# A fused linear-attention and multiplicative-FFN kernel: Strassen block products, an earlier weight product, and a list-scheduled order

## The chip, the cores and the metric

The kernel runs on one core of one Trainium2 chip. The metric is the device time of one execution in microseconds (us). Every median below is over the executions of that kernel in one comparison (three to eight). Executions come in a fast and a slow state; for one core an execution counts as slow when it is over 1.5% above the fastest of its kernel.

Engines: PE is TensorE (matmuls and transposes), ACT is ScalarE, DVE is VectorE, POOL is GpSimd, SP is SyncE, whose queue issues the DMAs. PEld is PE's weight load.

## The reference

Eight batches of 576 tokens, 8 heads of 64 features: q, k, v are (8, 8, 576, 64) in float32. The attention is a linear one, and its result feeds a multiplicative FFN.

```python
q_s = exp(q - max(q, -1)); q_s /= sum(q_s, -1)          # softmax over the features of a token
k_s = exp(k - max(k, 2));  k_s /= sum(k_s, 2)           # softmax over the tokens
kv  = einsum('bhsd,bhse->bhde', k_s, v)                 # 64x64 per head
x   = einsum('bhsd,bhde->bhse', q_s, kv)                # -> 4608 tokens x 512 features
a, b = x @ w1, x @ w2                                   # 4608 x 1024 each
out  = ((a * b) @ w3) @ w_out                           # 4608 x 512
```

## The kernel before

It computes in float16 with float32 accumulation, and multiplies w3 @ w_out once into `W3O`, so that the last two products become one. Tokens go through in nine chunks of 512. For each chunk, `s1` makes a block of 128 of the 1024 features with eight matmuls of 512 columns, ACT copies the first product out of PSUM, DVE multiplies it into the second; `s2` makes the output. The pieces of later batches' attention are woven by hand between the feature blocks.

```python
def load_qkv(b, which, hf):                     # half of the heads of q, k or v of a batch
    t = slot([SP, 4, R * D])                    # 96 partitions, 4 runs of 1536 B in each
    nc.sync.dma_start(out=t, in_=src[b, 4*hf:4*hf+4].rearrange("h (p r) d -> p h (r d)", r=R))

def piece_t(b, p):                              # transpose the normalised q on PE, DVE copies it out
    pt = pAtt([P, R, SP], F16)
    for r in range(R):
        nc.tensor.transpose(pt[:, r, :], eqn[:, r]..., ident[:SP, :SP])
    nc.vector.tensor_copy(out=qsT, in_=pt...)

def s1(j, fb):
    pa = pAB()
    for ct in range(4):
        nc.tensor.matmul(pa, lhsT=w1sb[qt][:, ct, fo:fo + P], rhs=xT[ct][:, t0:t0 + 512], ...)
    nc.scalar.copy(out=a16, in_=pa)
    pb = pAB()
    for ct in range(4):
        nc.tensor.matmul(pb, lhsT=w2sb[qt][:, ct, fo:fo + P], rhs=xT[ct][:, t0:t0 + 512], ...)
    nc.vector.tensor_tensor(out=ab, in0=pb, in1=a16, op=ALU.mult)

# order: q, k, v of batch 0; w1, w2; chunk 0; then w3 @ w_out; then chunks 1 to 8, in each of them
# the attention of batch j+1, the exponentials of batch j+2 and the loads of batch j+3
```

The softmax here doesn't subtract the row's maximum and nothing guards it: scores larger than these inputs give would overflow.

## Time and profile before

Median 292.8 us (291.25 to 293.15). In a window table a row is a stretch of time, and after it the busy time of each engine with its number of instructions, the granted PE clock, the busy share of the 16 DMA engines and what they moved in GB/s.

The first lines are from the page of the profile: PE's busy time, then the span in 40 slices of 7.26 us (a digit is the busy tenths of a slice) for PE, its granted clock and DMA, and the chain of work that ended last, by engine.

```profile
...
PE 245.5 (85%) x1440; PEld 125.1 (43%) x1440; DVE 140.0 (48%) x268; ACT 124.3 (43%) x217; POOL 79.2 (27%) x64
...
PE   0218997739693399999999999999999999999993
...
PEclk9999999998888579999999999999999999999999
DMA  7999999990139999949946965971121112121124
...
PE 79%; DMA 8%; ACT 5%; DVE 3%; issue 1%; SPq 1%; DVEq 0%; ACTq 0%
...
```

Counting the slices from 0, PE starts late, has holes in slices 6 to 13, and is full from slice 14 on. DMA is busy early and has room later. The next view is a table of stretches of the same execution.

```profile
...
core 0: us, PE busy (x) PEld busy (x) DVE busy (x) ACT busy (x) POOL busy (x), PEclk, DMA share, GB/s
40.00:60.00 20.00, 16.37 (x116) 8.67 (x115) 6.22 (x10) 6.93 (x10) 4.54 (x4) 1.00 1.07 296
80.00:100.00 20.00, 10.00 (x48) 4.27 (x47) 6.52 (x12) 9.08 (x16) 4.87 (x4) 0.76 0.78 191
120.00:140.00 20.00, 20.00 (x130) 10.57 (x129) 13.48 (x27) 11.52 (x22) 8.70 (x6) 1.00 0.75 181
160.00:180.00 20.00, 20.00 (x129) 10.50 (x128) 12.03 (x26) 10.33 (x19) 7.28 (x5) 1.00 0.72 179
...
```

From 110 us on PE is busy all the time at full clock. The waits of PE (line, what it waited for, total us, times, longest) show what the early holes are:

```profile
...
PE att L152 <- POOL v_0_75 L127: 10.0, 1, 10.0
PE att L180 <- DVE qsT L172: 7.8, 2, 5.4
PE att L169 <- POOL eqn L138: 7.7, 3, 3.9
PE pab L204 <- ACT a_880 L201: 5.9, 1, 5.9
PE att L235 <- ACT w_611 L232: 4.5, 1, 4.5
...
```

These are single long waits for the first batches and for w3. The first line is the time before PE's first matmul. A useful account of PE can be made from the starts of its matmuls. Take the time from one matmul's start to the next: up to the full-rate duration it is *work*; what the granted clock explains beyond that is *cold*; the rest is *waits*. For the full-rate duration the Trainium skill, "TensorE: Matmul & The Clock Gate", Part 1, gives columns / 2.4 + 2.5 ns; the spacing of 0.216 us at 512 columns in this trace agrees, and so does its half clock after idle stretches (the granted clock is 0.50 from 92 to 96 us, 0.76 on average from 80 to 100 us). About 5 us of tail and the time before the first matmul come on top. For this kernel: 231.1 us work, 6.6 cold, 38.4 waits, first matmul at 10.0 us.

### The profile page before, as it was taken

To read this page: it belongs to the slowest core of one execution; us is meant where nothing else is said; L and a number is where in the kernel's file an instruction comes from. 1 tells how busy PE (TensorE), PEld (TensorE's weight loads), DVE (VectorE), ACT (ScalarE), POOL (GpSimd) and SP (SyncE) were. 2 spreads that over 40 slices of the span, in tenths; PEclk is the share of its full clock that TensorE was granted. 3 is DMA by queue.
4 is the path that set the end of the run, shared out by engine and by line. 5 is a ranking of instruction groups with operands and counts; after the bars stand their busy time and mean duration, and the time that the engine had idled before them with its cause. 6 is when DMAs were issued, how large, how long until landed. Compare 5 with 4: busy or idle time off the path is not lost.

```text
span 290.4 us, 3985 instructions
## 1 busy us (share of the span) xinstructions
PE 245.5 (85%) x1440; PEld 125.1 (43%) x1440; DVE 140.0 (48%) x268; ACT 124.3 (43%) x217; POOL 79.2 (27%) x64
## 2 busy tenths in 40 slices
PE   0218997739693399999999999999999999999993
PEld 0115444415441155555555455455555544444441
DVE  0344453231733468476476476657745434333441
ACT  3426542263344558556464456445622332121200
POOL 1461702305503456354125405505400000000000
PEclk9999999998888579999999999999999999999999
DMA  7999999990139999949946965971121112121124
GB/s 182 254 326 391 357 351 282 261 250 15 41 97 236 256 256 256 228 118 220 280 129 156 257 149 128 261 208 38 48 62 38 36 47 64 36 73 38 55 76 121
DMA packets 31443, 48.49 MB, mean 167 GB/s; under 512 B 2240, under 2 KB 24768, under 8 KB 31424
## 3 DMA queue, kind: packets, MB, share of 16 engines
q1 hardware_dynamic: 31424, 48.24, 62.3%
q8 instruction: 11, 0.18, 0.3%
q14 instruction: 8, 0.07, 0.1%
HBM read 38.80 MB, written 9.44 MB: 166 GB/s over the span
## 4 chain that ended last, share of the span: by engine, by line
PE 79%; DMA 8%; ACT 5%; DVE 3%; issue 1%; SPq 1%; DVEq 0%; ACTq 0%
PE pab L204 22%; PE pab L198 21%; PE po L215 21%; DMA st<-in_q_dram 8%; PE po L243 5%; PE att L152 4%; PE att L180 3%; PE att L169 2%; ACT eq L120 2%; ACT ek L111 1%; PE att L235 1%; DVE ds L134 1%; SPq L78 1%; DVE osb L218 0%; ACT w_542 L232 0%
## 5 line engine op out<-in xcount | busy, mean ns | idle before, releaser
L138 POOL TENSOR_TENSOR eqn<-eq,dr 96x768 f16<-96x768 f16 x32 | 46.8, 1470 | 98.9 <-DVE dr L136 57.5
L134 DVE TENSOR_REDUCE ds<-eq 96x12 f32<-96x768 f16 x32 | 30.0, 936 | 44.2 <-ACT eq L120 44.1
L215 PEld LDWEIGHTS <-abT 128*128 128x128 f16 x288 | 27.6, 99 | 30.5 <-issue 1.1
L218 DVE TENSOR_SCALAR osb<-po 128x512 f32<-128x512 f32 x36 | 24.8, 688 | 27.2 <-PE po L215 26.2
L120 ACT ACTIVATE eq<-st 96x768 f16<-96x768 f32 x32 | 26.4, 843 | 11.8 <-DMA st<-in_q_dram 11.8
L111 ACT ACTIVATE ek<-st 96x768 f16<-96x768 f32 x32 | 25.8, 843 | 8.5 <-DMA st<-in_k_dram 8.5
L169 PE MATMUL att<-ident,eqn 96*128 96x96 f16 x192 | 14.8, 219 | 7.7 <-POOL eqn L138 7.7
L152 PEld LDWEIGHTS <-ek 96*128 96x128 f16 x192 | 14.5, 108 | 13.9 <-ACT ek L111 7.0
L169 PEld LDWEIGHTS <-eqn 96*128 96x128 f16 x192 | 12.4, 105 | 13.9 <-POOL eqn L138 8.7
L152 PE MATMUL att<-v_0_75,ek 96*128 96x130 f16 x96 | 8.8, 254 | 10.0 <-POOL v_0_75 L127 10.0
L172 DVE COPY qsT<-att 128x576 f16<-128x576 f16 x32 | 14.2, 450 | 0.7 <-PE att L169 0.6
L204 PEld LDWEIGHTS <-w_0_85 128*128 128x128 f16 x72 | 7.4, 103 | 16.0 <-issue 8.6
L127 POOL CAST v_0_75<-st 96x1536 f16<-96x1536 f32 x8 | 11.7, 1461 | 9.2 <-DMA st<-in_v_dram 8.8
L215 PE MATMUL po<-W3O_93,abT 128*128 128x512 f16 x36 | 13.9, 386 | 0.0
L215 PE MATMUL po<-W3O_96,abT 128*128 128x512 f16 x36 | 13.9, 386 | 0.0
L215 PE MATMUL po<-W3O_95,abT 128*128 128x512 f16 x36 | 13.9, 385 | 0.0
L215 PE MATMUL po<-W3O_94,abT 128*128 128x512 f16 x36 | 13.9, 385 | 0.0
L215 PE MATMUL po<-W3O_97,abT 128*128 128x512 f16 x36 | 13.7, 381 | 0.0
L215 PE MATMUL po<-W3O_98,abT 128*128 128x512 f16 x36 | 13.6, 379 | 0.0
L215 PE MATMUL po<-W3O_99,abT 128*128 128x512 f16 x36 | 13.6, 379 | 0.0
L215 PE MATMUL po<-W3O_100,abT 128*128 128x512 f16 x36 | 13.6, 379 | 0.0
L204 PE MATMUL pab<-xT_71,w_0_85 128*128 128x512 f16 x18 | 7.3, 404 | 5.9 <-ACT a_880 L201 5.9
(265 smaller groups left out, 507.3 us busy)
## 6 DMA issues: line engine op xcount, KB each, us to landing
st<-in_k_dram SPq DMA_DIRECT2D x16, 576.0 KB, 9.7
st<-in_v_dram SPq DMA_DIRECT2D x16, 576.0 KB, 8.5
st<-in_q_dram SPq DMA_DIRECT2D x16, 576.0 KB, 10.0
st<-in_moe_w_dram SPq DMA_DIRECT2D x16, 512.0 KB, 7.7
out_dram<-osb SPq DMA_DIRECT2D x24, 192.0 KB, 2.3
out_dram<-osb SPq DMA_DIRECT2D x24, 128.0 KB, 2.3
st<-in_moe_w_out_dram SPq DMA_DIRECT2D x4, 512.0 KB, 5.5
out_dram<-osb SPq DMA_DIRECT2D x24, 64.0 KB, 2.0
```

What stands on the lines that cost most here:

```text
L111: nc.scalar.activation(out=ek.rearrange("p r h d -> p h r d"), in_=t[:, o:o + 2].rearrange("p h (r d) -> p h r d", r=R), func=AF.Exp)
L120: nc.scalar.activation(out=eq.rearrange("p r h d -> p h r d"), in_=t[:, o:o + 2].rearrange("p h (r d) -> p h r d", r=R), func=AF.Exp)
L134: nc.vector.tensor_reduce(out=ds, in_=eq, axis=AX.X, op=ALU.add)
L138: nc.gpsimd.tensor_tensor(out=eqn.rearrange("p r h d -> p (r h) d"), in0=eq, in1=dr[:, :, None].broadcast_to([SP, 2 * R, D]), op=ALU.mult)
L152: nc.tensor.matmul(kvp[:, pp, :].rearrange("p (h e) -> p h e", h=2), lhsT=ek[:, r].rearrange("p h d -> p (h d)"), rhs=v16buf[b % 2][:, 2 * ...
L169: nc.tensor.transpose(pt[:, r, :], eqn[:, r].rearrange("p h d -> p (h d)"), ident[:SP, :SP])
L172: nc.vector.tensor_copy(out=qsT, in_=pt.rearrange("p r s -> p (r s)"))
L198: nc.tensor.matmul(pa, lhsT=w1sb[qt][:, ct, fo:fo + P], rhs=xT[ct][:, t0:t0 + CH], start=(ct == 0), stop=(ct == N_CT - 1))
L204: nc.tensor.matmul(pb, lhsT=w2sb[qt][:, ct, fo:fo + P], rhs=xT[ct][:, t0:t0 + CH], start=(ct == 0), stop=(ct == N_CT - 1))
L215: nc.tensor.matmul(po, lhsT=abT[(j, ft)][:, tb * P:(tb + 1) * P], rhs=W3O[ft], start=(ft == 0), stop=(ft == N_FT - 1))
L218: nc.vector.tensor_scalar(out=osb, in0=po, scalar1=ISC, scalar2=None, op0=ALU.mult)
L243: nc.tensor.matmul(wps, lhsT=w3Ts[ft][:, gt, :], rhs=wosb[gt // 2][:, gt % 2, :], start=(gt == 0), stop=(gt == N_FT - 1))
```

## The change

Its intent: (1) multiply x with w1 and w2 with seven block products instead of eight for all tokens but the first 512, (2) do w3 @ w_out first, while the attention's inputs load, (3) transpose q of batches 2 to 7 by DMA instead of by PE, (4) let a list scheduler, given assumed durations, choose each engine's order. The seven products need sums of weights (made once, DVE and ACT), sums of tokens (POOL from group 2 on), and per block seven evictions from PSUM and a product on POOL where there were four evictions for as many tokens.

```diff
+class Planner:                     # greedy list scheduler over PE, ACT, DVE, POOL, SP
+    def run(self): ...             # DMA modelled as one pipe: begin, nbytes / rate, + 1100 ns
+    GROUPS = [(512, 320), (1152, 448), (2048, 448), (2944, 448), (3840, 384)]  # start, half h
-    stage = ... bufs=9             # slots for loads
+    tiles("st", 6, [P, 1536], F32)
+    tiles("pa", 1, [P, 1024], F32, psum)   # the one PSUM buffer of the attention
...
+        load((which, b, hf), SP * 1536 * 4, 300.0, ...)       # bytes, assumed bytes/ns
...
+            if by_pe:              # batches 0 and 1
+                nc.tensor.transpose(...)   # into pa, then a DVE copy
+            else:
+                    nc.sync.dma_start_transpose(out=qsT.tile, in_=eqn.tile...)
...
+    def t_comb(i, prio, eng):      # t3 = b22-b12, t2 = t3+b11, t1 = b12-b11, t4 = b21-t2
...
+    def wino(i, fb, prio, tt, ts): # one block: 128 features, 2h tokens
+        x1: X  = w1_0 b11          e1: s1 = X (ACT)
+        w : W  = w1_1 b21          k1: c11 = W + s1 (DVE)
+        x2: X += wc_1 t2           e2: u2 = X (ACT)
+        x3: X += wc_0 t1           e3: u4 = X (ACT)
+        v1: V  = wc_2 t3           k2: c22 = V + u4 (DVE)
+        x4: X += wc_3 b22          k3: ab[h:2h] = X * c22 (DVE)
+        v2: V += w2_1 t4           k4: c21 = V + u2 (DVE)
+                                   k5: ab[0:h] = c11 * c21 (POOL)
...
+    make_w3o()
+    attention(0, True, -20.0)
...
+        attention(b, b < 2, 8.0 * first[b] - 9 + 0.5 * (b % 2))
+    plan.run()
```

(The body of `wino` is put in short form here; each line of products is two matmuls of h columns.)

## The prediction

> **What bounds it now.** The chain of waits is 79% PE (L204 22%, L198 21%, L215 21%). By stretches: from 110 to 280 us PE is 100% busy at full clock (steady state); there eight 512-column matmuls take 1.73 us (0.216 us each). At full rate PE has only about 230 us of work: 576 L198/L204 matmuls 124.4, 288 L215 62.2, w3@w_out 17.4, attention 8 x 3.3. The other 60 us are start-up and starvation: PE idles until 10 us and is 0.27/0.75 busy to 30 us, waits for w3 between 43 and 66 us (14.8 of 23 busy), and for q, k, v at 87-99 us (2.5 of 12 busy, DMA share 1.01), with half-rate matmuls (0.43 us apart) after.
>
> **What the change does.**
> 1. Strassen on 4096 of 4608 tokens: per block of 128 features, 14 matmuls over h columns for 16. The Trainium skill, "TensorE: Matmul & The Clock Gate" (Part 1), gives N/2.4 + 2.5 ns back to back; the trace's 0.216 us at 512 agrees. Estimate 112 x (0.136 + 3 x 0.189 + 0.163) = 97 us for 110.6: **-13.6 us**, all on the critical path.
> 2. Transposes of batches 2-7 go from PE to DMA: **-6 us** of PE, -11 us of DVE copies off the path. 24 more transfers of 147 KB; "DMA: Bandwidth & Descriptors" (Latency and other measured facts) gives 261 GB/s, about 0.6 us each; this trace has none.
> 3. w3@w_out moves to the front, where PE was idle: loading 6 MB at ~390 GB/s plus batch 0 at 256 GB/s lasts to about 33 us, and most of its 17 us fit in there. **Largest gain.**
> 4. Added, meant to stay hidden: ACT 3 evictions per block (~0.53 us), DVE 4 (~0.62), POOL 1 product and token combinations. In a 896-token group estimated PE 38, ACT 32, DVE 29, POOL 27 us. ACT is 80-85% full, so some bubbles. A block's chain (4 PE, 3 ACT steps in one bank) is about 4.9 us; two banks give 2.45 us per block against 2.65 of its matmuls: just enough, as other PE work fills in.
>
> **Sum.** PE work falls to about 211 us. Batches arrive every 13.8 us when DMA is full: batch 0 at 33, w1/w2 at 44, batch 1 at 57, batch 3 at 85. Plain group ~38-52, its output product to ~60, group 1 from ~63, group 2 from ~92 (after batch 3). Remaining PE then: 63.6 + 18.2 (Strassen groups) + 46.7 (output product) + 11.5 = 140 us, plus 4-5% bubbles, 3.5 us of tail, and 2.4 us that runs exceed the profiled span. **Predicted 247 us, 236 to 266.** Chances: faster 0.96, same 0.03, slower 0.01.
>
> **What would show each step.** (1) Strassen matmuls total ~97 us with 0.19 us spacing at 448 columns. (2) No PE transposes of eqn for batches 2-7; DMA transposes landing in ~3 us. (3) w3/w_out matmuls over by ~33 us and the plain group starting near 38. (4) PE 93-97% busy from 92 us to the end; waits of PE for ACT's evictions short (<0.5 us) but many. DMA saturated to ~140 us; PE gaps at 60-63 and 85-92 us.
>
> **What would make it wrong.** DMA transposes much slower than a plain copy, delaying the loads behind them on the one SP queue. The order is planned from assumed durations; where real ones differ, in-order engines block each other: PE at 85% in the steady state would mean ~262.

## The result, and the profile after

Median 280.5 us (277.56 to 283.01, four executions, one of them slow); before, in the same comparison, 292.3 us. The ratio is 0.9565, with a 95% interval of 0.9501 to 0.9629. Ratios here are the mean time of one kernel's fast runs over that of the other's of the same rounds, so not quite the ratio of the medians. The output is correct. It is faster, but the predicted range of 236 to 266 us missed it.

The page after: the busy time of PE, the same slices (6.98 us each) with POOL added, and the chain by engine.

```profile
...
PE 234.3 (84%) x1344; PEld 122.1 (44%) x1344; DVE 164.2 (59%) x302; ACT 164.0 (59%) x298; POOL 145.2 (52%) x120
...
PE   1586862799946999894999995999999999999992
...
POOL 2213246204566378869869689989694221222200
PEclk9999795599995799998899999999999999999999
DMA  7999995699999999999999999931311212212154
...
PE 52%; DMA 28%; DVE 6%; ACT 4%; issue 4%; POOL 3%; SPq 0%; DVEq 0%; ACTq 0%; POOLq 0%
...
```

PE's share of the chain fell from 79% to 52%, and DMA's rose from 8% to 28%. DMA is now full from slice 8 to slice 25 without a break, up to about 182 us. The same stretches as before:

```profile
...
40.00:60.00 20.00, 11.49 (x57) 5.55 (x58) 17.32 (x29) 13.85 (x25) 7.73 (x4) 0.66 0.73 219
80.00:100.00 20.00, 14.28 (x89) 9.12 (x89) 13.86 (x28) 12.00 (x22) 11.23 (x10) 0.74 1.12 267
120.00:140.00 20.00, 15.91 (x74) 7.15 (x73) 10.31 (x19) 16.08 (x33) 17.14 (x12) 0.91 1.15 248
160.00:180.00 20.00, 16.34 (x83) 7.79 (x81) 10.45 (x19) 15.45 (x34) 18.00 (x14) 1.00 1.12 244
...
```

In the stretches from 120 and 160 us PE was full before; now it is busy 15.9 and 16.3 of 20 us, with DMA above 1.1 and POOL at 17 and 18 of 20. The waits of PE:

```profile
...
PE px L419 <- ACT ab L413: 6.8, 4, 5.1
PE pa L326 <- ACT xt L388: 6.8, 6, 3.3
PE pa L377 <- DVE qsT L332: 6.3, 6, 3.0
PE px L568 <- POOL tt L544: 3.9, 2, 2.5
PE px L419 <- POOL ab L413: 3.4, 4, 1.6
...
PE pa L377 <- DMA qsT<-eqn: 1.1, 1, 1.1
...
```

Of the first line, 5.1 us are the time before the first matmul. Of the rest none is large. They are spread over the casts of w3 (L419), the one attention buffer (L326, waiting for ACT's copies), the copies of the transposes (L377) and the token sums (L568). The DMA issues, with KB of each and the median us from issue to landing:

```profile
...
st<-in_k_dram SPq DMA_DIRECT2D x16, 576.0 KB, 8.2
...
st<-in_q_dram SPq DMA_DIRECT2D x16, 576.0 KB, 10.7
...
qsT<-eqn SPq DMA_TRANSPOSE x24, 7.6
```

A transpose was predicted to land in about 3 us and takes 7.6 in the median (2.5 to 12.6). The five issued after the last load had landed, from 177 us on, took 2.5 to 2.9: it is beside the loads that a transpose takes so long.

The account of PE and the arrival of the inputs, worked out from the traces (a batch has landed when the last packet of its q, k and v has):

| | before | predicted | after |
|---|---|---|---|
| PE work, us | 231.1 | 211 | 211.4 |
| PE cold, us | 6.6 | - | 8.8 |
| PE waits, us | 38.4 | - | 48.7 |
| batch 0 landed at | 16.8 | 33 | 38.9 |
| batch 1 landed at | 58.7 | 57 | 69.0 |
| batch 3 landed at | 108.8 | 85 | 101.4 |
| batch 7 landed at | 193.7 | 139.8 (57 + 6 x 13.8) | 175.6 |
| us per batch, 1 to 7 | 22.5 | 13.8 | 17.8 |
| plain group starts | - | 38 | 53.2 |
| group 1 starts | - | 63 | 90.2 |
| group 2 runs (first matmuls at 124.9, then a stall for token sums on POOL) | - | 92 | 131.2 |
| from the landing of batch 0, 1, 3 to the first product of the plain group, group 1, 2 | - | 5, 6, 7 | 14.3, 21.2, 23.5 |
| from group 2 to the end of the span | - | about 150 | 147.9 |

So the PE work fell by 19.7 us, as predicted, and the waits and cold time rose by 12.5 us. From the end of group 2's stall to the end the time is as predicted (140 us of PE, 4 to 5% of bubbles, 3.5 us of tail make about 150). The miss lies before group 2. The longer interval of before is not a limit of its DMA, whose share was 0.7 there.

### The profile page after: what moved, and what is told of

Its sections match the earlier page's. It is cut to its first block, busy times and chain, and to the rows that moved or that the text cites. A ratio compares the mean times of both kernels' runs of the same rounds, so it can differ in the third digit from the quotient of the medians.

```text
span 279.1 us, 4087 instructions
## 1 busy us (share of the span) xinstructions
PE 234.3 (84%) x1344; PEld 122.1 (44%) x1344; DVE 164.2 (59%) x302; ACT 164.0 (59%) x298; POOL 145.2 (52%) x120
## 4 chain that ended last, share of the span: by engine, by line
PE 52%; DMA 28%; DVE 6%; ACT 4%; issue 4%; POOL 3%; SPq 0%; DVEq 0%; ACTq 0%; POOLq 0%
PE px L568 18%; PE pp L634 14%; PE pp L568 13%; DMA st<-in_q_dram 11%; DMA st<-in_moe_w_dram 7%; DMA qsT<-eqn 4%; DMA st<-in_k_dram 3%; PE pa L377 3%; PE pa L351 3%; POOL tt L544 2%; ACT eq L300 2%; DMA out_dram<-osb 2%; DMA st<-in_moe_w_out_dram 1%; ACT xt L388 1%; DVE ds L306 1%
## 5 line engine op out<-in xcount | busy, mean ns | idle before, releaser
L634 PE MATMUL pp<-W3O,ab 128*128 128x512 f16 x288 | 77.7, 379 | 0.8 <-DVE c L593 0.7
L593 DVE TENSOR_TENSOR c<-pp,u 128x448 f16<-128x448 f32 (+2 forms) x80 | 45.6, 575 | 35.3 <-ACT u L589 23.2
L311 POOL TENSOR_TENSOR eqn<-eq,ds 96x768 f16<-96x768 f16 x32 | 49.0, 1541 | 29.4 <-DVE ds L308 17.6
L619 POOL TENSOR_TENSOR ab<-c,c 128x448 f16<-128x448 f16 (+2 forms) x40 | 38.3, 958 | 49.1 <-DVE c L593 48.9
L568 PEld LDWEIGHTS <-wc 128*128 128x128 f16 x320 | 31.6, 99 | 37.6 <-issue 9.2
L568 PE MATMUL px<-tt,wc 128*128 128x448 f16 (+2 forms) x160 | 41.7, 349 | 4.2 <-POOL tt L544 3.9
L634 PEld LDWEIGHTS <-ab 128*128 128x128 f16 x288 | 27.9, 98 | 25.7 <-issue 1.3
L589 ACT COPY u<-px 128x448 f32<-128x448 f32 x48 | 25.5, 537 | 23.0 <-PE px L568 17.1
L568 PEld LDWEIGHTS <-w 128*128 128x128 f16 x240 | 23.7, 99 | 21.7 <-issue 1.8
L644 ACT ACTIVATE osb<-pp 128x512 f32<-128x512 f32 x33 | 19.4, 600 | 21.0 <-PE pp L634 21.0
L593 DVE TENSOR_TENSOR c<-pp,s 128x448 f16<-128x448 f32 (+2 forms) x40 | 23.0, 579 | 13.7 <-PE pp L568 8.8
L593 DVE TENSOR_TENSOR ab<-px,c 128x448 f16<-128x448 f32 (+2 forms) x40 | 23.3, 582 | 5.0 <-PE px L568 2.7
L377 PE MATMUL pa<-qsT,kv 128*128 128x288 f16 x64 | 14.2, 306 | 8.8 <-DVE qsT L332 6.3
L568 PE MATMUL pp<-tt,wc 128*128 128x448 f16 (+2 forms) x80 | 20.5, 341 | 1.1 <-DVE c L593 1.1
L590 ACT COPY u<-px 128x320 f32<-128x320 f32 (+1 forms) x32 | 14.3, 452 | 12.0 <-PE px L568 7.4
L568 PE MATMUL pp<-tt,w 128*128 128x448 f16 (+2 forms) x80 | 20.2, 336 | 0.7 <-DVE c L593 0.7
```

Source lines behind the costliest of these rows:

```text
L311: nc.gpsimd.tensor_tensor(out=eqn.tile.rearrange("p r h d -> p (r h) d"), in0=eq.tile.rearrange("p r h d -> p (r h) d"), in1=ds.tile[:, 1] ...
L377: nc.tensor.matmul(xp.tile[:, 224 + hh * HS:224 + (hh + 1) * HS], lhsT=kv2.tile[:, p, :], rhs=qsT.tile.rearrange("p r s -> p (r s)")[:, hh ...
L568: nc.tensor.matmul(ps.tile[:, 0:h], lhsT=lhs(c), rhs=rhs(c), start=first and c == 0, stop=c == 1, skip_group_check=not first)
L589: return lambda: nc.scalar.copy(out=dst.tile, in_=src.tile[:, 0:h]) if h == HM else \
L593: return lambda: nc.vector.tensor_tensor(out=dst(), in0=ps.tile[:, 0:h], in1=other.tile[:, 0:h], op=op)
L619: nc.gpsimd.tensor_tensor(out=ab.tile[:, 0:h], in0=c11.tile[:, 0:h], in1=c21.tile[:, 0:h], op=ALU.mult)
```

## The experiments

Eighteen kernels ran. All change the kernel after. "Wrong" kernels compute a wrong output and keep every wait. Where only the code of an operation was made smaller, the planner saw the same durations, so each engine's order is that of the kernel after. Where a task, a buffer or a rate changed, the planner ordered everything anew; such a comparison carries the luck of another order as well, and the runs below show that this can be 5 to 7 us.

Ratios are to the kernel before in the same call.

### First call: order, transposes, Strassen, loads

The rivals: A, the DMA supply of tokens is slower than predicted (loads at the real rate, DMA transposes on the same 16 engines); B, the order is planned with wrong rates; C, Strassen's own side work takes back its gain.

**All transposes on PE** (`pe_transposes`): PE gets 6.1 us more work, DMA loses 24 transposes.

```diff
-        attention(b, b < 2, ...)
+        attention(b, True, ...)
```

> All eight batches transposed on PE again (24 fewer DMA transposes, 6 us more PE work, 11 us more DVE copies); the order is planned anew. In the trace of the changed kernel the transposes' 256-byte packets took 25 us of all 16 DMA engines, and the loads ended near 183 us. Supply theory (until 183 us the DMA engines are full and the batches of q, k, v arrive late): the loads end 10 to 20 us earlier and the time falls to 262-272. Order theory (the order was planned for loads of 300 GB/s, so in-order engines sit behind late ones): little fall, 276-284. Side-engine theory (the block products' extra work on ACT, DVE, POOL holds PE): DVE gets more work, so 281-287.

Measured: 278.6 us (277.04 to 282.02), ratio 0.9536 (0.9487 to 0.9586), correct. Batch 7 landed 14 us earlier (161.5), and waits and cold fell by 9.8 us, to 47.7; of that 6.1 were paid for as PE work. Batch 3, for which group 2 waits, landed 6 us earlier (95.2). The DMA transposes do delay the loads, but taking them away buys almost nothing (0.9536 against 0.9565).

**Planner told slower DMA rates** (`plan_rates`): only the order changes.

```diff
-  q, k, v 300.0   w1/w2 380.0   w_out 390.0   w3 400.0   transposes 150.0
+  q, k, v 240.0   w1/w2 300.0   w_out 310.0   w3 310.0   transposes 140.0
```

> The same work; only the DMA rates that the list scheduler assumes are changed to about what the trace shows (q, k, v 240 instead of 300 bytes per ns, weights 300 to 310 instead of 380 to 400, transposes 140), so only the order of instructions changes. Order theory: falls by 8 us or more, to 272 or less. Supply theory: within 2% of the changed kernel, 275-285.

Measured: 287.4 us (286.88 to 288.25), ratio 0.9859 (0.982 to 0.9898), correct: slower than the kernel after. B falls in the form that better rates would give a better order. Even for the true order the planner had no good answer at these rates: its own plan ended at 283 us.

**Plain products instead of Strassen** (`no_strassen`): the groups stay, each half group takes eight matmuls per feature block; no weight or token sums.

```diff
-            wino(i, fb, 8.0 * i + fb, tt, ts)
+            halves(i, fb, 8.0 * i + fb)     # like plain(), for h columns, twice
```

> The same groups, loads, transposes and scheduler, but the first two products the plain way: 16 products for 14 per feature block, about 13.8 us more PE work, no weight or token combinations, 1 ACT and 1 DVE operation per half instead of 3 and 4 per pair. If PE bounded throughout: +13 us, 293. Supply theory: the extra PE work partly fills waits before 183 us, so only what is PE-bound after it pays: +2 to +8 us, 282-288. Side-engine theory: equal or faster than the changed kernel, 280 or less.

Measured: 278.7 us (278.3 to 279.32), ratio 0.956 (0.9523 to 0.9597), correct. This is the time of the kernel after (0.9565), with 13.9 us more PE work (225.3). So as the kernel stands **Strassen is worth nothing**, and the gain over before comes from the rest of the change. The account: waits 35.7 instead of 48.7, cold 5.2 instead of 8.8. Two of its stretches:

```profile
...
120.00:140.00 20.00, 17.98 (x114) 10.11 (x113) 10.84 (x20) 13.75 (x24) 7.43 (x6) 1.00 1.14 255
160.00:180.00 20.00, 19.39 (x123) 10.92 (x121) 11.98 (x22) 13.98 (x28) 9.26 (x7) 1.00 0.92 199
...
```

PE is busier (18.0 and 19.4 us), with the DMA share in the first as high as in the kernel after. Input arrives 4 to 7 us earlier (batch 3 at 94.5 us, batch 7 at 171.3), and the plain products fill the time with work where Strassen's wait. At 183 us, when PE has become full in both, 17.7 feature blocks are left here and 20.7 with Strassen; at 16 or 14 matmuls of 0.189 us each (all counted as 448 columns) that is 53.6 and 54.8 us. Strassen has saved nothing by then, and the rest is even. The planner had seen most of this: run by itself, without the chip, it ends this kernel at 255.4 us and the kernel after at 253.3, so by its own durations Strassen was worth 2 us.

**Loads of q, k, v as 128 partitions x 4608 B** (`wide_loads`, wrong: the layout does not fit the attention; same bytes, same order).

```diff
-             src[...].rearrange("h (p r) d -> p h (r d)", r=R))
+             src[...].rearrange("h (p r) d -> (h p) (r d)", r=18), dst=lambda t: t[:, :1152])
```

> Wrong result on purpose: q, k, v come with the same bytes but as 128 partitions of 4608 contiguous bytes instead of 96 partitions of 1536-byte pieces, into the same slots; instruction order and everything else are the same (only a memset of the slots' last columns is added). Estimate from the trace: 28.3 MB at 350 instead of 240 GB/s is 37 us less DMA time. Supply theory: loads end by 155 us, time 252-262. Side-engine theory: 272 or more. The order theory expects a fall too, as the loads then come as planned, so it is plan_rates that tells those two apart.

Measured: 266.8 us (266.3 to 267.65), ratio 0.9152 (0.9107 to 0.9196). The packet records say why: q, k and v go as 18,432 packets of 1,536 B, 105.5 ns each in the kernel after, which on 16 engines is 122 us, or 15.2 per batch and 233 GB/s. As 4,608-B packets they take 202 ns each, 78 us in all and 365 GB/s. A is right for a part: 13.7 us (12.0 by the ratios). PE waits fell to 36.0, batch 7 landed at 153.0. PE is nearly full in two of the stretches that were looked at before (from 140 to 160 us it is busy 17.8), and DMA no longer is:

```profile
...
120.00:140.00 20.00, 19.97 (x115) 10.41 (x113) 17.60 (x34) 17.05 (x31) 15.80 (x13) 0.91 0.76 197
160.00:180.00 20.00, 19.82 (x122) 10.58 (x120) 17.57 (x33) 16.04 (x33) 19.08 (x15) 1.00 0.27 63
...
```

But batch 3 landed at 85.0 us, just as predicted, and group 2 still began only at 111.6 us instead of 92. So late loads are not all of it.

### Second call: one buffer, slots, and combinations of these

From batch 0 in the trace of the kernel after: its four pairs go through the single attention buffer one by one, 2.7 us apart, and the fp32 slots are held by the weight sums. Three edits were to remove such waits: transposes of batches 0 and 1 into the `px` banks; weight sums read from the float16 copies, so that slots come free earlier; both with PE transposes; and without Strassen as a control.

```diff
-                pa = Buf("pa")            # in by_pe
+                pa = Buf("px")
-            a, b = va(ba.tile), vb(bb.tile)
+            a, b = w1sb[qt], w2sb[qt]
```

> One edit: the PE transposes of batches 0 and 1 write the two px banks instead of the one pa buffer that the x products of the same batch also need. In the changed kernel the four pairs of batch 0 run one after the other, 2.7 us each (transpose 0.64, copy 0.46, product 0.64, eviction 0.70 of one buffer), and batches 0 and 1 took 14 and 20 us from landing to the first product that needs them. Theory one-buffer (this chain starts the groups late): pairs 1.4 to 1.8 us apart, the plain group starts by 49 us instead of 53.2, time 272-277. Supply theory alone: 278-283.

Measured: 286.0 us (284.57 to 287.08), ratio 0.983 (0.9766 to 0.9893), correct. Slower.

> px_transposes, and the third weights are combined from the two f16 copies instead of the fp32 staging slots, so a slot is free after its cast. Theory slots (the combinations on DVE hold the six slots and so delay the loads of batch 1; in no_strassen, which has none, batch 1 was complete at 62.7 us and not 69.0): batch 1 complete by 64 us, group 1 earlier by 4 to 6 us and the time 3 to 7 us under px_transposes. If slots do not matter: within 2 us of it.

Measured: 291.0 us (285.57 to 292.61), correct; three of four executions, and the profiled one, were slow, so there is no ratio. Inconclusive in size, but no gain.

> px_f16_combine with all transposes on PE, that is without the DMA transposes. Supply theory: with the two other waits gone the earlier batches (14 us earlier by the last one in pe_transposes) pay at last: 258-268. If PE's own chains still bound the groups: 268-275.

Measured: 281.3 us (279.9 to 284.81), ratio 0.9666 (0.9573 to 0.976), correct. The plain group began at 49.3 us and batch 7 landed at 159.1, both earlier than in the kernel after, and the end did not move.

> px_f16_pe with plain products (no combinations at all). Strassen saves 13.8 us of PE work. If it pays once the start is mended: 8 to 14 us slower than px_f16_pe. If its cost on the side engines and the start still eats it: within 3 us of px_f16_pe, or faster.

Measured: 285.4 us (284.28 to 289.31), ratio 0.98 (0.9734 to 0.9865), correct.

In all four the planner made a new order, so they do not price the single edit. What they show: removing the wait that looks longest in the trace does not move the end, and an earlier landing by itself does not either.

### Third call: Strassen's sums, with the order kept

`tiny_tokens` cuts the token sums to 8 columns, `tiny_weights` the weight sums; both are wrong and in the same order.

```diff
-                    out=o, in0=a, in1=b, op=op)
+                    out=o[:, :, 0:8], in0=a[:, :, 0:8], in1=b[:, :, 0:8], op=op)
```

> Wrong result on purpose: the combinations of the tokens (4 per group, 1.85 us each on POOL, on DVE for group 1) write 8 columns of each half only; order and waits of all instructions stay. By our account of the changed kernel PE loses 7 us at 120-140 us and 5 us at 160-180 us, where the plain version loses 2.4 and 1.0. Theory token latency (each group's second product waits for POOL after its tokens are complete): both stretches shrink to 1-3 us and the time falls by 5 to 9 us, to 271-276. Otherwise 278-282.

Measured: median 283.0 us (278.6 to 284.91), ratio 0.9727 (0.9683 to 0.9771), which fits the five executions from 282.3 to 284.9 us; the profiled one was the fastest, and beside it four of the six count as slow. Against 280.5 us for the kernel after, no gain, of uncertain size. PE no longer waits for `tt`, but its waits in the trace stay at 48.7 us in total: the wait for DMA transposes (L377 for `qsT<-eqn`) rose from 1.1 to 5.1 us. One wait was replaced by another that ends at nearly the same time.

> Wrong result on purpose: the combinations of the third weights (4 on DVE, 2 on ACT per quarter) write 8 columns only; order and waits stay. Theory slots (they keep DVE 84% busy at 40-60 us, hold the staging slots, and so delay batch 1, complete at 69.0 us): batch 1 complete by 65 us, first product of group 1 by 85 us (90.2 in the changed kernel), time 3 to 7 us less, 273-277. Otherwise 278-282.

Measured: 279.4 us (277.81 to 281.26), ratio 0.9586 (0.9533 to 0.9639). No gain.

> Wrong result on purpose: no_strassen with the wide loads (4608-byte pieces on 128 partitions). Beside wide_loads (266.8) it gives Strassen's worth when the loads are fast. If the late loads alone ate Strassen's 13.9 us: 8 to 14 us slower than wide_loads, 275-281. If Strassen's own waits ate them: 263-270.

Measured: 261.7 us (260.87 to 262.16), ratio 0.8973 (0.8944 to 0.9003), wrong. With fast loads Strassen *costs* 5 us: 266.8 against 261.7, the ratios' intervals do not touch. PE waits are 20.9 without and 36.0 with it.

> Wrong result on purpose: wide loads, and both kinds of combinations cut to 8 columns. If slow loads and combinations are the causes, what is left is PE's 211 us, 10 us of start and end, and the waits of batch 0 (about 20 us): 246-254, about what was predicted for the change. If it stays over 258, a cause is missing from the list.

Measured: 269.6 us (269.3 to 270.09), ratio 0.925 (0.9222 to 0.9277), wrong. This one is spoilt: the memsets that initialise the shortened buffers took some 13 us of DVE at the start, and the casts of w_out waited behind them. It tells nothing about the sums.

### Fourth and fifth call: the load of the side engines, and the square

A Strassen block has three ACT and four DVE evictions and one POOL product, where two plain half blocks have two and two evictions. The cuts, in the same order: `wide_light_blocks` makes these eight operations 8 columns wide; `wide_light_pool` does so with POOL's casts of v, its normalisation of q (except the first use of a buffer) and the token sums from group 2 on (their buffers are set by POOL in the first microseconds, which leaves the landings as they were, though in `wide_light_both` DVE's first cast of w_out beside it took 3.69 us instead of 0.69; the plain group begins at 44.5 us there and at 44.3 in `wide_loads`, so it is not passed on); `wide_light_both` has both; all with the wide loads. All three are wrong.

```diff
-                nc.scalar.copy(out=dst.tile[:, 0:h], in_=src.tile[:, 0:h])          # and k1 to k5
+                nc.scalar.copy(out=dst.tile[:, 0:8], in_=src.tile[:, 0:8])
-                    out=eqn... , in0=eq... , in1=ds...broadcast_to([SP, 2 * R, D])
+                    out=eqn...[:, :, c], in0=eq...[:, :, c], in1=ds...broadcast_to([SP, 2 * R, 8])
```

> Wrong on purpose: wide loads (266.8 us), and on GpSimd the casts of v, the normalisation of q and the token combinations are cut to 8 columns, except the first use of each buffer; order unchanged. If GpSimd's load makes the long way from landing to finished features (16 to 35 us with wide loads), the latency falls under 15 us, and PE's gaps from 36 to under 22 us: 250 to 254 us. If GpSimd is only one of several nearly coincident waits, 261 to 267 us.

Measured: 262.1 us (260.18 to 262.3), ratio 0.8969 (0.8924 to 0.9013). PE waits 33.4 instead of 36.0. The way from landing to finished features did not shorten as expected (16 to 34 us): where PE is fed in time, that way is only the queue ahead of it.

> Wrong on purpose: wide loads, and all eight evictions of each Strassen block (three on ScalarE, four on VectorE, one on GpSimd) cut to 8 columns; order unchanged. If the three dependent evictions of a block are what turns Strassen's saving into waits (15 us more gaps than without Strassen, with wide loads), PE's gaps fall from 36 to about 21 us: 250 to 254 us. If not, 263 to 267 us.

Measured: 262.7 us (260.82 to 263.67), ratio 0.9003 (0.8959 to 0.9048). PE waits 30.7.

> Wrong on purpose: both cuts together. If the side engines' load as a whole is what is left beside the loads, PE's gaps fall to 10 to 15 us: 238 to 245 us, near the prediction of 247. If what is left is the fixed order or the arrival of loads and transposes, at least 258 us.

Measured: 255.4 us (254.25 to 255.91), ratio 0.8756 (0.8723 to 0.8789). PE waits 26.0, of which 22.1 lie before 80 us, as many as in `wide_loads` (22.0). From then on PE is nearly full:

```profile
...
80.00:100.00 20.00, 19.93 (x146) 13.37 (x145) 10.21 (x40) 12.87 (x36) 4.28 (x16) 0.97 1.00 242
120.00:140.00 20.00, 19.97 (x139) 11.53 (x138) 8.54 (x35) 11.05 (x28) 2.96 (x11) 1.00 0.99 321
160.00:180.00 20.00, 20.00 (x108) 10.37 (x107) 4.90 (x26) 6.74 (x24) 2.77 (x13) 1.00 0.21 50
...
```

**The missing corner** (`light_both`): the same cuts with the real loads, wrong.

> Wrong on purpose: the cuts of wide_light_both with the real loads. If loads and side engines add up (13.7 and 11.4 us with wide loads), 268 to 271 us. If the loads hide the side work, 274 to 280 us. If side work was what held the loads' slots back, under 266 us.

Measured: 282.3 us (281.62 to 282.92), ratio 0.9708 (0.9665 to 0.9751). Nothing gained; by the ratios 4 us lost. By the same account its waits are 2 us shorter than in the kernel after and its cold time 4 us longer (13.0; the granted clock is 0.923 over the span, 0.943 in the kernel after). Its DMA slices and the same stretches:

```profile
...
DMA  7999995699999999999999999942211212122154
...
```

```profile
...
80.00:100.00 20.00, 13.77 (x91) 9.45 (x90) 9.63 (x28) 9.93 (x23) 2.72 (x9) 0.66 1.12 267
120.00:140.00 20.00, 13.66 (x61) 6.31 (x61) 6.52 (x19) 11.92 (x29) 3.39 (x13) 0.89 1.14 239
160.00:180.00 20.00, 16.85 (x79) 8.11 (x78) 5.82 (x20) 11.87 (x29) 2.99 (x12) 0.91 1.14 248
...
```

POOL is down from 17 to 3.4 of 20 us in the stretch from 120 us, and PE is busy less than in the kernel after (13.7 against 15.9). DMA is full up to the same slice, and batch 7 lands at 177.0 us (after: 175.6). With the real loads the side engines are hidden behind DMA.

**Plain products with the same freedom** (`plain_wide_light`): no Strassen, wide loads, POOL's attention work and the two evictions of each block cut; wrong.

> Wrong on purpose: no Strassen, wide loads (261.7 us), and the same cuts as wide_light_both: on GpSimd the casts of v and the normalisation, of the plain groups the copies on ScalarE and the products on VectorE. If side work costs only Strassen, because its evictions and combinations fill the engines, 259 to 262 us, and Strassen is worth 4 to 6 us (255.4) once the side engines are free. If plain products gain as much, 250 to 254 us, and Strassen is worth nothing on any footing.

Measured: 260.4 us (259.68 to 261.7), ratio 0.8948 (0.8905 to 0.8991). Plain products gain 1.3 us from the cut, Strassen 11.4.

Together, medians in us:

| | Strassen | plain products | Strassen is worth |
|---|---|---|---|
| real loads, real side work | 280.5 | 278.7 | -1.8 (nothing, within the intervals) |
| real loads, light side work | 282.3 | - | - |
| wide loads, real side work | 266.8 | 261.7 | -5.1 |
| wide loads, light side work | 255.4 | 260.4 | +5.0 |

The first median, 280.5, holds a slow execution. By the ratios, times 291.5 us, the last column is -0.1, -5.2 and +5.6. The columns differ in their planned order, so a few us of a row may be order; within a column the order is the same (and between the rows of plain products as well).

**A correct candidate** (`pe_rates`): transposes on PE, planner told the measured rates.

```diff
-  q, k, v 300.0   w1/w2 380.0   w_out 390.0   w3 400.0      attention(b, b < 2, ...)
+  q, k, v 240.0   w1/w2 300.0   w_out 310.0   w3 310.0      attention(b, True, ...)
```

> Correct: all transposes on PE, and the planner told the measured rates of the loads (240 for q, k and v, 300 and 310 for the weights); its own plan then ends at 264.5 us. If the plan is now near the truth, 266 to 273 us, faster than both kernels. If the waits lie in what the plan leaves out (engines slowed by one another, half-clock matmuls), 277 to 285 us.

Measured: 278.5 us (276.24 to 284.85), ratio 0.9528 (0.9476 to 0.9581), correct. The plan said 264.5. So no correct kernel is clearly faster than the kernel after: `pe_rates`, `pe_transposes`, `no_strassen` and the kernel after lie within 1%.

## Why the prediction was wrong

Right: the direction; the PE work (211.4 us for 211); the time from the end of group 2's stall to the end (147.9 us for about 150); that most of w3 @ w_out fits into the idle start, though it ended at 39.7 us instead of 33.

**The step that failed first: "Batches arrive every 13.8 us when DMA is full: batch 0 at 33, w1/w2 at 44, batch 1 at 57".** They arrive every 17.8 us. The term took 256 GB/s for q, k and v and gave nothing of the 16 DMA engines to the transposes and the outputs. Measured in packet time of the 16 engines per batch: 15.2 us for q, k and v (105.5 ns a packet; before 101 ns) and 4.2 us for four transposes (1.06 us each where 0.6 was estimated), 19.4 together, at a share of 1.12 to 1.15 (the sum of packet times; it can exceed 1), which makes about 17 us, before any output. Batch 7 landed at 175.6 instead of 139.8 us. That the rate of the loads counts is shown by `wide_loads` (-13.7 us, by the ratios -12.0, in the same order). That from some 56 us on the DMA engines, and not the side work that was cut, set the pace of the landings is shown by `light_both`: the batches land at the same times and the end does not come earlier. Its cut leaves the exponentials, the row sums and the weight sums as they are.

The start was late as well: batch 0 by 6 us, batch 1 by 12. The 4,096-B packets of w3 ran at 307 GB/s where the prediction took some 390 for the weights, and from 44 to 52 us the DMA engines were almost idle (shares of 0.16 and 0.36 in the two halves). The load queue waited for one of the six slots, in part until DVE was through with weight sums (L476, L480). Without these sums (`no_strassen`, in another order) DMA was busy there, and batch 1 landed at 62.7 us instead of 69.0. `tiny_weights` (67.8) did not close the hole, so the length of the sums alone is not the reason. The kernel after, one line of its queue's waits, and `no_strassen`:

```profile
...
40.00:50.00 10.00, 2.98 (x22) 1.79 (x23) 8.39 (x15) 6.46 (x11) 7.31 (x4) 0.62 0.64 209
...
SPq L230 <- DVE wc L476: 8.6, 4, 3.7
...
40.00:50.00 10.00, 3.83 (x24) 2.21 (x24) 6.23 (x12) 5.86 (x10) 3.89 (x3) 0.50 1.10 324
...
```

**The same sum had a second term wrong: the way from a landing to the first product that needs it.** The prediction let it take 5, 6 and 7 us (batch 0 at 33, plain group at 38; batch 1 at 57, group 1 at 63; batch 3 at 85, group 2 at 92). Measured: 14.3, 21.2 and 23.5 us. Of the 32.9 us by which group 2's first matmul came late, 16.4 are the landing of batch 3 and 16.5 are this way. None of the cuts shortened it by more than half a microsecond: 23.0 us before group 2 in `light_both`, 26.6 in `wide_loads`, 26.9 in `wide_light_both`. In the last 23.5 us PE was busy for 21.6, with group 1 (itself late), outputs and attention; before group 1 it was busy for 14.6 of 21.2. The planner, run by itself, also lands batch 3 at 85.0 us and starts group 2 at 105.0, so the prediction's 92 was 13 us ahead of the plan too. What would shorten this way was not tested.

**The step that failed second: "-13.6 us, all on the critical path".** The size is right, 13.9 us less PE work, but it is not on the critical path. Up to about 180 us PE is fed by DMA, so a shorter product lengthens the wait for the next batch: `no_strassen` ends at the same time (in another order, with its input 4 to 7 us earlier, so this reading is in part argued). With fast loads it could count, but there the third step fails.

**Third: the added work was "meant to stay hidden", with "ACT is 80-85% full, so some bubbles".** With wide loads the added work is no longer hidden: Strassen then loses 5 us to plain products, and gains 5 when the side engines are relieved. A full cut is needed for that: from the 266.8 us of `wide_loads`, POOL's part and the evictions alone gave 4.7 and 4.2 us, both together 11.4. Neither the token sums nor the weight sums alone gave anything with the real loads.

The miss of 33.5 us can be walked along same-order kernels: 280.5 to 266.8 us by the loads (by the ratios 12.0 of these 13.7), 266.8 to 255.4 by the side work, and 8.4 us to the predicted 247 that no experiment removed. Of the waits in the last of these kernels 22.1 us lie in the first 80 us. PE runs there at a granted clock of 0.82 from 40 to 60 us (0.66 in the kernel after), and group 2 begins at 109.9 us, still 18 us later than predicted. That this start makes the 8.4 us is read from the trace and not tested. The walk has an order: the side work taken away first gives nothing.

The prediction's own warning named DMA transposes "much slower than a plain copy, delaying the loads behind them". They are slower, and they do delay the loads by 14 us (`pe_transposes`), but on PE they cost 6.1 us of work and the end moved by 2 us only. Its other warning, of a planned order against real durations, is open in size: three re-planned kernels (`plan_rates`, `px_transposes`, `no_strassen_px_pe`, the last with 20 us more PE work) were slower than the kernel after by 5 to 7 us, and none was faster by more than 1%. One instance of it is in the trace of the kernel after. At 81.5 us PE had finished a product of batch 1, but ACT, whose order put exponentials of batch 2 first, stood idle for 2.6 us until q of batch 2 landed at 82.5 us. It copied the product out at 84.06 us, and PE waited for the one buffer:

```profile
...
84.73 0.64 PE L326 MATMUL pa<-ident,eqn 96*128 96x96 f16 x6 [3.27 <-ACT xt L388]
...
```

With wide loads the longest wait of this kind is 0.8 us instead of 3.3.

In part open: why landings of batch 7 that are 14 to 17 us earlier (`pe_transposes`, `px_f16_pe`) do not bring the end forward as the wide loads do; both carry a new order and 6.1 us more PE work. Batch 7 is a poor measure: in the kernel after the group that needs it begins 55.7 us after its landing. Batch 3 came only 6.2 and 8.9 us earlier in these two kernels, and 16.4 in `wide_loads`.

## What to carry to other kernels

Work taken from the busiest engine counts only in the stretches where that engine is not waiting for input: first work out, stretch by stretch, when the input arrives, with the packet time of every transfer on the DMA engines (loads, transposes and stores together), and then how long the way from the landing to the first product takes. When waits of several engines end at nearly the same time, cutting one shows nothing; cut several at once, with the order kept, and test the combination on both sides of the change. A schedule made from assumed durations ended at 253 us by its own count and at 279 us on the chip, so its ranking of variants should be measured, not believed.

## What the Trainium skill lacked or had wrong

- "DMA: Bandwidth & Descriptors", Latency and other measured facts: it gives 261 GB/s for a DMA transpose. Here a transpose of 96 x 768 float16 (147 KB) took 1.06 us of all 16 engines, in 256-B packets of 29.5 ns in the mean, which is 139 GB/s, beside loads on the same engines, and landed in 7.6 us. After 182 us, with the loads over, the packets took 20.7 ns, 197 GB/s, and a transpose landed in 2.5 to 2.6 us. So most of the difference is the loads' doing, and what is left is a fourth.
- The same page, Specifications: it puts the smallest transfer for line rate at 512 B. Here 1,536-B packets over 96 partitions ran at 233 GB/s (243 before the change), and the same bytes as 4,608-B packets over 128 partitions at 365 GB/s. Packet size and partition count were changed together, but size alone does not explain it: the 1,024-B packets of w1 and w2, over 128 partitions, ran at 295 GB/s (339 before the change), faster than the 1,536-B ones over 96.
- "SBUF — State Buffer", SBUF: two separate sides: it says that GpSimd and VectorE (in its two-port modes, or with two SBUF inputs) share a port pair as an exclusive lock, the loser blocking fully. Nothing wrong there: the trace agrees that one is held up, and gives sizes. A POOL normalisation that takes 1.47 us elsewhere took 3.29 while three such DVE instructions passed (one of 32; the next longest took 1.75; POOL's is recorded as begun 0.09 us before the first of the three, so which had the ports first is not shown); the casts of weights on DVE took 0.65 to 0.68 us, and 1.99 beside two POOL normalisations. Of Strassen's costs this one, weight sums on DVE holding up POOL, was not in the prediction at all, and in this trace it is small. The timeline of the kernel after (start, duration):

```profile
...
41.25 1.99 DVE L457 CAST w<-st 128x1024 f16<-128x1024 f32 x1 [0.54 <-DMA st<-in_moe_w_dram]
...
44.50 3.29 POOL L311 TENSOR_TENSOR eqn<-eq,ds 96x768 f16<-96x768 f16 x1 [1.81 <-DVE ds L308]
44.59 0.67 DVE L468 TENSOR_TENSOR sw<-st 128x512 f32<-128x512 f32 x1
...
45.18 0.68 DVE L457 CAST w<-st 128x1024 f16<-128x1024 f32 x1
...
45.78 0.68 DVE L472 TENSOR_TENSOR sw<-sw,st 128x512 f32<-128x512 f32 x1
...
```
